# Attention and a mixing MLP in one kernel: the second batch's keys and queries turned by DMA transposes, and the order of the last product's tiles

## The chip, the cores and the metric

The kernel runs on one core of a Trainium2 chip. The metric is the device time of one launch in microseconds (us), the median of several runs. A core has TensorE (PE in the profile; its weight loads are PEld), VectorE (DVE), ScalarE (ACT), GpSimd (POOL) and SyncE (SP), and 16 DMA engines that all of its queues share. SP issues DMAs on the hardware queue that the profile calls q1, GpSimd on the software queue q0, ScalarE on q10.

## The reference

Eight batches of 384 tokens. First grouped-query attention (16 query heads on 4 key/value heads, head size 64), then a two-stage residual MLP with affine layers: a mix over tokens and an MLP over channels (1024 to 4096 to 1024).

```python
scores = (q @ k.transpose(0, 1, 3, 2)) / sqrt(64)      # k, v repeated 4 times over heads
attn   = exp(scores - max) / (sum + 1e-9)
x      = heads_to_columns(attn @ v)                    # (8, 384, 1024)
a1  = alpha1 * x + beta1
tok = einsum('ts,bsd->btd', w_tok, a1)                 # 384 x 384 over tokens
u   = x + lam * tok
a2  = alpha2 * u + beta2
ch  = maximum(a2 @ w_ch1, 0) @ w_ch2                   # 1024 x 4096, 4096 x 1024
out = u + lam * ch
```

## The kernel before

Everything is bf16 on TensorE with f32 sums. The order of instructions on each engine is the order of the program (a manual schedule); semaphores between engines come only from what reads and writes which buffer.

**Stages.** Batch 0's attention comes first, alone. Then `main(0)` and `main(1)` each do the channel MLP of one batch: a hidden product (phase 0: 32 rows of 128 hidden channels, 8 matmuls of L531 each, a relu into `hT`) and a second product (phase 1: 6 units of 32 matmuls of L569, evicted by VectorE at L576 and stored). After that come three calls of `pair`, which do two batches at once with seven half-size products for each product in place of eight, out of sums of blocks of the weights and of the operands (L722 is the hidden product, L786 the second one).

**Side work between matmuls.** `main` and `pair` are generators that yield after every four or eight matmuls. Between two yields the program puts pieces of other work from a plan: `put(stage, phase, unit, function, ...)`. So the attention of batch 1 runs inside phase 1 of `main(0)`, that of batch 2 inside phase 0 of `main(1)`, and so on. For one batch the attention is, by pairs of heads `p`: `scores` (L279 on TensorE, exp on ScalarE at L288 into `es`), `av` (L315, then four VectorE operations L320 to L330 that give `xr` and the operand `a1`), `tok` (L340, then L347 and L351 on VectorE into a buffer `a`, of which there are two), a store of `xr` into `out` (`spill`, L243 on SP) and a DMA transpose of `a` into `ops` (`a2_transpose`, L362 on SP). All scores of a batch need its keys and queries with the head dimension on the partitions: `kT` and `qT`. There is one `kT` and one `qT`, one buffer `k2` and one buffer `q_raw` that the loads fill, so the loads of batch b+1 wait until batch b's have been turned.

**Turning the heads.** There are two ways in the code. `k_transpose` and `q_transpose` (L255, L265) do it on TensorE, six 128x128 transposes into PSUM at a time, which VectorE copies out (L257, L267); batches 0 and 1 use it. `flip_k` (L172) and `flip_q` (L176) are DMA transposes on SP, from SBUF to SBUF; all later batches use them. For batch 1 the plan has the transposes at units 9, 24, 28, 32, 36 and 40 of phase 0 of `main(0)`. That phase has 60 units: the first four rows were begun in batch 0's attention and give one unit each, the other 28 rows two.

**Weights.** W1 comes in 16 chunks of two rows (256 columns, 512 KB in bf16) through a ring of six slots, by GpSimd's DMAs (`load_w1`, L185), which cast from f32: when a chunk has been used, the chunk six places on is loaded. After the last of W1 for batch 0, GpSimd issues 13 blocks of W2 (`load_w2`, L189, into `arena`), and then batch 2's k, q and v (`load_next`, L508). All of these go through q0 in that order.

**Relus.** In `main` a counter `exps` says which engine does a row's relu. An exp on ScalarE sets it to 2, each row takes one off, and while it is not below 0 the relu goes to VectorE (L542), otherwise to ScalarE (L540). The third and the sixth group of scores leave their last exp to be done later: it is put into `late`, and the next `av` issues it.

**The last product.** The last call of `pair` (`last`) ends with the product `o == 4`, in which each of three token tiles `ms` gets 16 matmuls, in two halves `h` of 8. The third token tile is held in two PSUM tiles, columns 0 to 383 and 384 to 511, and each is done by itself. When a tile has its 16th, VectorE multiplies it by lam (L794) and adds it to `ends` (L795), and SP stores it (L796).

Of the kernel before, what the change touches and what calls it, by code (L numbers as in the profile page):

```python
# [12 lines left out]
def kernel(  # L13
# [21 lines left out]
    nc = tc.nc  # L35
# [14 lines left out]
    NST = S // P  # L50
# [64 lines left out]
    def by_tok(ap):  # L115
        return ap.rearrange("(p st) d -> p st d", st=NST)
# [91 lines left out]
    late, exps = [], [0]  # L208
# [20 lines left out]
    def side(b):  # L229
# [175 lines left out]
        def av(p):  # L405
            av_piece(p, 0)
            av_piece(p, 1)
            while late:
                late.pop(0)()

        def tok_flip(p):
            tok(p)
# [18 lines left out]
        if not first:  # L431


            turns = {}
            if b == 1:
                turns = {5: [(to_all, 3, 0, 0), (load_row_set, 1, 1, 0)], 7: [(to_all, 3, 1, 1), (load_row_set, 2, 0, 1)],
                         9: [(k_transpose, 0)], 12: [(to_all, 1, 0, 2)], 14: [(to_all, 1, 1, 0), (load_row_set, 2, 1, 0)],
                         17: [(scale_beta,)], 20: [(to_all, 2, 0, 1)], 22: [(to_all, 2, 1, 0)],
                         24: [(q_transpose, 0, 2, "av")], 28: [(k_transpose, 2)]}
                for i in range(3):  # L440
                    turns[32 + 4 * i] = [(q_transpose, 2 + 2 * i, 2, "av")]
            if (b - NPL) // 2 > 0:
                at = {}

                def put(k, *m):
                    at.setdefault(k, []).append(m)

                for j in range(6):
                    put((0, 6, 12, 21, 26, 31)[j], scores3, j, j in (2, 5))
                for p in range(NP):  # L450
                    put((4, 10, 14, 18, 24, 29, 33, 35)[p], av, p)
                    put((8, 15, 17, 22, 27, 32, 36, 38 if b % 2 else 39)[p], tok_flip, p)
                    if by_pe(p):
                        put((36, 39, 41)[p - NP + 3], turn, p)
                return turns, at
            return turns, {
                0: [(scores3, 0)], 4: [(av, 0)], 6: [(scores3, 1)], 8: [(tok_flip, 0)], 11: [(av, 1)],
                13: [(scores3, 2, True)], 15: [(av, 2)], 16: [(tok_flip, 1)], 18: [(tok_flip, 2)], 19: [(av, 3)],
                21: [(scores3, 3)], 23: [(tok_flip, 3)], 25: [(av, 4)], 27: [(scores3, 4)], 29: [(tok_flip, 4)],
                31: [(av, 5)], 33: [(scores3, 5, True)], 35: [(av, 6), (tok_flip, 5)], 37: [(av, 7)],  # L460
                38: [(tok_flip, 6)], 41: [(tok_flip, 7)],
                **{39 + 4 * i - i // 2 * 2: [(turn, p)] for i, p in enumerate((5, 6, 7)) if by_pe(p)}}
# [207 lines left out]
    def pair(i):  # L670
        b0 = NPL + 2 * i
# [24 lines left out]
        last = i == NB - 1  # L696
# [12 lines left out]
        for g in range(NH // 2):  # L709
            X, Y, snap = {}, {}, {}  # L710
            for k, (o, e) in enumerate(SEQ1):
                t = 2 * g + e
# [51 lines left out]
        X = [c_banks(ms) if last else None for ms in range(NST)]  # L764
        snap = {}
        where = {2: (0, 0), 3: (0, 1), 7: (1, 1), 4: (1, 0)}
        for k, o in enumerate(PLACE2):
            whole = not last and o != 4
            for h in range(1 if whole else 2):
                for ms in range(NST):  # L770
                    if o == 4 and not last and 1 < 3 * h + ms < 5:
                        sum_w1(0, (5, 7, 6)[3 * h + ms - 2])
                    if last and (o, h) in ((6, 1), (7, 0)):
                        (lift_end if o == 7 else begin_end)(ms)
                    if last and (o, h, ms) == (7, 0, NST - 1):
                        X[ms] = [(c0, c1, pairs[sc].tile([P, 2, 512], f32, tag="sc", name="C", bufs=1)[:, 0, :c1 - c0])
                                 for sc, c0, c1 in (("sc1", 0, 384), ("sc2", 384, 512))]
                    if whole:
                        X[ms] = [(0, 512, acc.tile([P, 512], f32, tag="acc", name="C", bufs=2))]
                    elif not last and h == 0:  # L780
                        X[ms] = c_banks(ms)
                        pairs["held"] = ms == NST - 1
                    upto = NH if whole else 8 * h + 8
                    for (c0, c1, x), t in ((c, t) for c in X[ms] for t in range(8 * h, upto)):
                        slot, rhs = w2_slots[i, 4 * k + t // 4], w2_at[i, 4 * k + t // 4]
                        nc.tensor.matmul(out=x, lhsT=hid[:, t, LEFT2[o], ms * P:(ms + 1) * P],  # L786
                                         rhs=rhs[:, t % 4 * 512 + c0:t % 4 * 512 + c1],
                                         start=((not last or o in (1, 6, 7)) and t == 0), stop=(t == NH - 1),
                                         skip_group_check=True)
                        if t % 4 == 3 and ms == NST - 1 and c1 == 512 and not (o == 4 and slot >= RING):  # L790
                            free(slot)
                        if last and o == 4 and t == NH - 1:
                            e, v = ends[ms][:, c0:c1], spare(ms).bitcast(f32)[:, c0:c1]
                            tt(out=v, in0=x, in1=lam_t[:, c0:c1], op=MUL)  # L794
                            tt(out=e, in0=e, in1=v, op=ADD)  # L795
                            nc.sync.dma_start(out=by_tok(out[b0 + 1])[:, ms, c0:c1], in_=e)  # L796
                        if t % 4 == 3 and t < upto - 1 and c1 == 512:
                            q = 4 * ms + t // 4
                            if whole and o in (2, 6) and q in (2, 5, 8, 10):
                                sums_hid(o, (2, 5, 8, 10).index(q))  # L800
                            if t % 8 == 3 and later and (last or later[0][1] != 4):
                                flush(1)
                            yield 1
                    if k == ms == h == 0:
                        pad_free[:] = [RING + 1, RING + 2, RING]
                        pump()
                    if (whole or h == 1) and not (last and o == 4):
                        if o in (1, 6, 5):
                            q = ((1, 6, 5).index(o) * NST + ms) * 512
                            snap[o, ms] = snaps[:, q:q + 512]  # L810
                        else:
                            bb, dw = where[o]
                            t = snap[1, ms] if o == 7 else spare(ms).bitcast(f32)
                        for c0, c1, x in X[ms]:
                            if o == 1:
                                nc.scalar.copy(out=snap[o, ms], in_=x)
                            elif o in (6, 5):
                                tt(out=snap[o, ms], in0=x, in1=snap[1 if last or o == 6 else 6, ms], op=ADD)
                            elif o == 2 and last:
                                tt(out=t, in0=x, in1=lam_t[:, :512], op=MUL)  # L820
                            else:
                                base = {2: 1, 3: 1 if last else 5, 7: 5, 4: 6}[o]
                                tt(out=t[:, c0:c1], in0=x, in1=snap[base, ms][:, c0:c1], op=ADD)
                            if o == 7 and not last:
                                tt(out=snap[6, ms], in0=x, in1=snap[6, ms], op=ADD)
                        if o not in (1, 6, 5):
                            later.append((scaled, o, b0 + bb, ms, dw, t))
                    if last and o in (2, 6) and (h, ms) in ((0, 1), (0, 2), (1, 0), (1, 1)):
                        sums_hid(o, [(0, 1), (0, 2), (1, 0), (1, 1)].index((h, ms)))
                    yield 1  # L830
# [5 lines left out]
    with tc.manual_schedule(engines=order):  # L836
# [131 lines left out]
        def put(ps, phase, at, *m):  # L968
            plan.setdefault((ps, phase, at), []).append(m)

        def put_all(ps, phase, table, at=lambda u: u):
            for u, ms in table.items():
                for m in ms:
                    put(ps, phase, at(u), *m)

        def put_flips(ps, phase, b, places):
            for u, m in zip(places, ((flip_k, b), *((flip_q, b, i, 2) for i in range(0, NP, 2)))):
                put(ps, phase, u, *m)

        turns, at = side(1)  # L980
        put_all(0, 0, turns)
        put_all(0, 1, at)
        put_flips(0, 1, 2, (34, 36, 37, 42, 43))

        put(0, 1, 45, load_next, 3)
# [71 lines left out]
```

## Time and profile before

| | us |
|---|---|
| median of 3 runs | 740.92 (740.89 to 741.25) |
| the profiled execution, its own time | 740.56 |
| its span, first to last instruction | 738.8 |
| TensorE busy | 731.5 (99%) |
| VectorE busy | 516.9 (70%) |
| ScalarE busy | 324.1 (44%) |
| GpSimd busy | 163.5 (22%) |
| DMA moved | 151.32 MB, 205 GB/s on average |

The granted TensorE clock is 0.999 over the span. Times inside the span count from its first instruction. In the profiled execution the hidden product of batch 0 runs from about 36 to 75 us, its second product to about 130, those of batch 1 to 242, and the three pairs to the end. In a row of the timeline the columns are start, duration, engine, line, operation, out<-in, count, and in brackets the engine's idle time before it with what ended it. In a row of the DMA view's queues they are packets, MB, and the time that the packets took as a share of the 16 engines' time, which can exceed 100% because an engine has more than one packet under way.

### The profile page before, as it was taken

The numbers are of one execution on the slowest core, as the hardware profiler recorded it, in microseconds if no ns is written. First come the engines' busy times: TensorE is split into PE (matmuls) and PEld (weight loads), VectorE is DVE, ScalarE is ACT, GpSimd is POOL, SyncE is SP. The second block draws the span as 40 slices with busy tenths as digits, with TensorE's granted clock in tenths as the row PEclk, the third lists the DMA queues.
The fourth block names the chain that finished last, engine by engine and source line by source line (L and its number), as shares of the span: only waits on it lengthen the run. The fifth ranks groups of instructions, "written<-read, shape, count | busy, mean of one in ns | idle before, by whom it ended". The sixth has DMA issues, their size and how long they took to land.

```text
span 738.8 us, 14511 instructions
## 1 busy us (share of the span) xinstructions
PE 731.5 (99%) x5769; PEld 418.8 (57%) x5769; DVE 516.9 (70%) x995; ACT 324.1 (44%) x467; POOL 163.5 (22%) x211
## 2 busy tenths in 40 slices
PE   8999999999999999999999999999999999999997
PEld 5866555566555566655555566655555566654444
DVE  7763366467587889749777988847968988762354
ACT  7632431444333566653334366664343266660000
POOL 9434221420000232211013244020002222000011
PEclk9999999999999999999999999999999999999999
DMA  9999999999899999999989999998989999937965
GB/s 184 194 202 200 207 209 175 185 191 199 204 258 281 177 218 212 268 249 205 297 197 197 202 149 191 204 246 198 274 236 172 211 127 145 172 117 261 293 182 103
DMA packets 218017, 151.32 MB, mean 205 GB/s; under 512 B 88660, under 2 KB 197060, under 8 KB 217948
## 3 DMA queue, kind: packets, MB, share of 16 engines
q0 software_dynamic: 120304, 64.60, 66.6%
q1 hardware_dynamic: 97100, 85.39, 42.9%
q8 instruction: 45, 0.74, 0.4%
q10 hardware_dynamic: 544, 0.39, 0.2%
q14 instruction: 24, 0.20, 0.1%
HBM read 154.84 MB, written 38.27 MB: 261 GB/s over the span
## 4 chain that ended last, share of the span: by engine, by line
PE 95%; DVE 2%; DMA 1%; ACT 0%; issue 0%; DVEq 0%
PE C L786 30%; PE X L722 17%; PE h L531 10%; PE ch L569 10%; PE Y L722 8%; PE sc L279 5%; PE Z L722 4%; PE sc L315 4%; PE sc L340 3%; DMA ops<-a 1%; PE h L223 1%; PE tok L340 1%; PE av L315 0%; PE warm L841 0%; PE tp L265 0%; ACT hT L288 0%
## 5 line engine op out<-in xcount | busy, mean ns | idle before, releaser
L288 ACT ACTIVATE es<-sc 128x1024 bf16<-128x1024 f32 x126 | 121.4, 1023 | 155.9 <-PE sc L279 144.8
L786 PE MATMUL C<-w,arena 128*128 128x512 bf16 (+2 forms) x744 | 168.0, 372 | 0.0
L786 PEld LDWEIGHTS <-arena 128*128 128x128 bf16 x1040 | 94.8, 98 | 100.5 <-issue 5.1
L727 ACT ACTIVATE hT<-X,bias 128x384 f32<-128x384 f32 x144 | 83.7, 581 | 61.6 <-PE X L722 54.9
L722 PEld LDWEIGHTS <-w 128*128 128x128 bf16 x768 | 75.1, 98 | 50.0
L516 POOL DMA_DIRECT2D out_dram<-hT x33 | 28.7, 871 | 284.3 <-DVE hT L687 106.3
L569 PE MATMUL ch<-arena,hT 128*128 128x512 bf16 x384 | 90.8, 379 | 0.0
L185 POOL DMA_DIRECT2D w<-in_moe_w_ch_dram x68 | 62.8, 964 | 98.4 <-PE X L722 34.4
L531 PE MATMUL h<-ops,w 128*128 128x384 bf16 (+1 forms) x480 | 83.3, 327 | 0.8 <-DVE hT L542 0.7
L722 PEld LDWEIGHTS <-pad 128*128 128x128 bf16 x576 | 56.4, 98 | 37.2
L722 PE MATMUL X<-ops,w 128*128 128x384 bf16 x384 | 70.2, 326 | 0.0
L722 PE MATMUL X<-ops,pad 128*128 128x384 bf16 x384 | 70.2, 326 | 0.0
L786 PE MATMUL C<-pad,arena 128*128 128x512 bf16 (+2 forms) x296 | 69.9, 373 | 0.0
L531 PEld LDWEIGHTS <-w 128*128 128x128 bf16 x480 | 45.4, 98 | 30.4 <-issue 2.7
L569 PEld LDWEIGHTS <-hT 128*128 128x128 bf16 x384 | 34.8, 98 | 36.8 <-issue 2.5
L347 DVE TENSOR_TENSOR xr<-sc,xr 128x384 f32<-128x384 f32 x56 | 30.9, 552 | 23.4 <-PE sc L340 23.4
L315 PEld LDWEIGHTS <-es 128*128 128x128 bf16 x1008 | 38.2, 97 | 12.4
L340 PEld LDWEIGHTS <-wtokT 128*128 128x128 bf16 x576 | 37.5, 98 | 11.8 <-DVE a L330 0.8
L279 PE MATMUL sc<-qT,kT 64*128 64x384 bf16 (+2 forms) x576 | 42.0, 272 | 0.8 <-DVE xr L323 0.3
L320 DVE RECIPROCAL rinv<-sc 128x6 f32<-128x6 f32 x56 | 10.7, 192 | 44.3 <-PE sc L315 44.1
L315 PE MATMUL sc<-v,es 128*128 128x65 bf16 x1008 | 39.8, 193 | 0.0
L722 PE MATMUL Z<-ops,w 128*128 128x384 bf16 x192 | 39.0, 326 | 0.0
(138 smaller groups left out, 911.0 us busy)
## 6 DMA issues: line engine op xcount, KB each, us to landing
w<-in_moe_w_ch_dram POOLq DMA_DIRECT2D x68, 512.0 KB, 10.3
w<-w2s SPq DMA_DIRECT2D x60, 512.0 KB, 4.3
pad<-w2s SPq DMA_DIRECT2D x24, 512.0 KB, 8.1
out_dram<-xr SPq DMA_DIRECT2D x56, 192.0 KB, 6.1
out_dram<-hT POOLq DMA_DIRECT2D x33, 256.0 KB, 5.7
arena<-in_moe_w_ch_dram POOLq DMA_DIRECT2D x16, 512.0 KB, 20.0
w2s<-arena SPq DMA_DIRECT2D x28, 256.0 KB, 5.0
q_raw<-in_q_dram POOLq DMA_DIRECT2D x28, 192.0 KB, 10.4
```

The lines of the kernel that those rows point to most:

```text
L185: nc.gpsimd.dma_start(out=w1[:, w1_slots[c]], in_=w1src[:, :, c * CW * P:(c + 1) * CW * P])
L279: nc.tensor.matmul(out=sc[:, hh, k % 4:k % 4 + n], lhsT=kT[r, 2 * p // G, BLK[hh][sk], :], rhs=qT[r, p, st:st + n, :], start=True, stop=True)
L288: nc.scalar.activation(out=e, in_=sc, func=EXP, scale=scale_qk)
L315: nc.tensor.matmul(out=av[:, hh, sq, :], lhsT=ess[k // 4][:, m % 2, k % 4, :], rhs=vb[:, sk, hk, :], start=(sk == 0), stop=(sk == NST - 1))
L340: nc.tensor.matmul(out=ps[:, tt, :], lhsT=wtokT[:, st, tt * P:(tt + 1) * P], rhs=a1s[p][:, st, :], start=(st == 0), stop=(st == NST - 1 an ...
L347: nc.vector.tensor_tensor(out=u, in0=ps, in1=u, op=ADD)
L516: nc.gpsimd.dma_start(out=at, in_=o, accum_op=ADD)
L531: nc.tensor.matmul(out=ps[:, :n], lhsT=w1[:, w1_slots[c], dt, j * P:(j + 1) * P], rhs=a2T[:, dt, :n], start=(dt == 0), stop=(dt == NDT - 1))
L569: nc.tensor.matmul(out=ps, lhsT=hT[:, nt, ms * P:(ms + 1) * P], rhs=w2[:, row(nt)[0], row(nt)[1], cs], start=(i == 0), stop=(i == NNT - 1))
L722: nc.tensor.matmul(out=ps, lhsT=tb[g, o][:, dt, e * P:(e + 1) * P], rhs=opb(LEFT1[o])[:, dt], start=(o in (1, 2, 7) and dt == 0), stop=(dt ...
L727: nc.scalar.activation(out=snap[o, e], in_=ps, func=IDENT, bias=hi if o == 5 else lo)
L786: nc.tensor.matmul(out=x, lhsT=hid[:, t, LEFT2[o], ms * P:(ms + 1) * P], rhs=rhs[:, t % 4 * 512 + c0:t % 4 * 512 + c1], start=((not last o ...
```

## The change

Batch 1's `k_transpose` and `q_transpose` leave the plan, and `flip_k` and `flip_q` for batch 1 enter it: all of k at unit 50 of phase 0 of `main(0)`, the first and second quarter of q at units 54 and 58, the third and fourth at units 3 and 9 of phase 1. In `av`, a put-off exp sets the relu counter to 1 instead of the 2 that the exp itself sets. In the last product's `o == 4`, the first half is done for two token tiles only, the third tile gets all its 16 matmuls at the end, and the store of its columns 384 to 511 is issued by ScalarE.

```diff
@@ av
             while late:
                 late.pop(0)()
+                exps[0] = 1
@@ side
             if b == 1:
                 turns = {5: [(to_all, 3, 0, 0), (load_row_set, 1, 1, 0)], 7: [(to_all, 3, 1, 1), (load_row_set, 2, 0, 1)],
-                         9: [(k_transpose, 0)], 12: [(to_all, 1, 0, 2)], 14: [(to_all, 1, 1, 0), (load_row_set, 2, 1, 0)],
-                         17: [(scale_beta,)], 20: [(to_all, 2, 0, 1)], 22: [(to_all, 2, 1, 0)],
-                         24: [(q_transpose, 0, 2, "av")], 28: [(k_transpose, 2)]}
-                for i in range(3):
-                    turns[32 + 4 * i] = [(q_transpose, 2 + 2 * i, 2, "av")]
+                         12: [(to_all, 1, 0, 2)], 14: [(to_all, 1, 1, 0), (load_row_set, 2, 1, 0)],
+                         17: [(scale_beta,)], 20: [(to_all, 2, 0, 1)], 22: [(to_all, 2, 1, 0)]}
@@ pair
             whole = not last and o != 4
+            tail = last and o == 4
             for h in range(1 if whole else 2):
-                for ms in range(NST):
+                for ms in range(NST - (tail and not h)):
...
-                    for (c0, c1, x), t in ((c, t) for c in X[ms] for t in range(8 * h, upto)):
+                    for (c0, c1, x), t in ((c, t) for c in X[ms]
+                                           for t in range(0 if tail and ms == NST - 1 else 8 * h, upto)):
...
-                            nc.sync.dma_start(out=by_tok(out[b0 + 1])[:, ms, c0:c1], in_=e)
+                            (nc.scalar if c0 else nc.sync).dma_start(out=by_tok(out[b0 + 1])[:, ms, c0:c1], in_=e)
@@ the plan
         put_all(0, 1, at)
+        put_flips(0, 0, 1, (50, 54, 58))
+        put(0, 1, 3, flip_q, 1, 4, 2)
+        put(0, 1, 9, flip_q, 1, 6, 2)
         put_flips(0, 1, 2, (34, 36, 37, 42, 43))
```

`put_flips(stage, phase, b, places)` puts `flip_k(b)` at the first place and `flip_q(b, 0, 2)`, `flip_q(b, 2, 2)`, ... at the following ones, as many as there are places.

## The prediction

> **What bounds the kernel now.** I read the page's busy shares first, then the chain of waits, then the weight loads of the first batch and the DMA engines under them, and last the end of the span.
>
> ```profile
> PE 731.5 (99%) x5769; PEld 418.8 (57%) x5769; DVE 516.9 (70%) x995; ACT 324.1 (44%) x467; POOL 163.5 (22%) x211
> PE 95%; DVE 2%; DMA 1%; ACT 0%; issue 0%; DVEq 0%
> ```
>
> TensorE is the bound and hardly ever stops: between 30 us and the end only two gaps exceed 0.1 us, 0.30 at 108.70 and 0.66 at 181.32. An instruction taken from it is worth its own time, provided nothing else becomes late. The chain, in the stretch where the six groups of transposes lie, shows their price:
>
> ```profile
> 51.26 2.61 PE h L531 x16
> 54.21 2.61 PE h L531 x16
> 57.16 2.61 PE h L531 x16
> ```
>
> Sixteen matmuls (two hidden rows) take 2.61 us, but these stretches start 2.95 apart: one group of six transposes is 0.34 us. Now the DMA engines in the same stage (the queue rows of the DMA view, 46 to 66 us, then 86.5 to 90, then 93.4 to 95.8; packets, MB, sum of packet times):
>
> ```profile
> q0 software_dynamic: 7779, 3.92, 144.7%
> ...
> q0 software_dynamic: 728, 0.72, 124.3%
> ...
> q0 software_dynamic: 376, 0.37, 91.8%
> q1 hardware_dynamic: 377, 0.10, 30.0%
> ```
>
> q0 is GpSimd's queue (W1, W2, next q, k, v), q1 is SP's. In the first row W1 alone moves in 512-byte packets: 20 us x 16 engines / 7779 = 41 ns each. In the second W2's 1024-byte packets alone take 3.5 x 16 / 728 = 77 ns. In the third one transpose of an a tile (128x384 bf16, 384 packets of 256 bytes) runs beside W2: the queues take turns one for one (376 to 377), and a pair costs 2.4 x 16 / 377 = 102 ns. So a transposing packet adds 25 ns to what waits on q0. Beside the 384-byte packets of v and q, 114.2 to 114.9 us, a pair is 56 ns where such a packet alone is 33 (30 to 32 us): 23 ns added. Transposes with the engines to themselves (133.9 to 134.9) pass 1080 packets in 1 us, 15 ns each. The engines have no free time here: the page's DMA share stands at 9 tenths.
>
> How close is W1 to late? The sixteenth chunk (its issue and the matmuls in the timeline, then its landing in the DMA view):
>
> ```profile
> 59.41 0.87 POOL L185 DMA_DIRECT2D w<-in_moe_w_ch_dram  x1 [2.08 <-PE h L531]
> 62.89 12.58 PE L531 MATMUL h<-ops,w 128*128 128x385 bf16 x76
> w<-in_moe_w_ch_dram POOLq DMA_DIRECT2D x1, 512.0 KB, 11.2
> ```
>
> It is issued at 59.41 and lands 11.2 later, at 70.65. The run of 76 matmuls ends issuing at 75.30, and the chunk holds the last 16 of them: needed at 72.69. Its slack is 2.04 us. Chunks land every 2.65 us while TensorE without transposes wants one every 2.61: the transposes sit in time that the DMA engines need anyway.
>
> **The change, part by part.** *Transposes off TensorE.* Six groups x 0.34 = 2.04 us of matmul time, and six evictions of about 0.555 us (L257, L267) on VectorE, which waits there for TensorE anyway. By itself that brings the end of the hidden stage forward by 2.04, exactly to where the sixteenth chunk arrives: 70.65 + 2.61 = 73.3.
>
> *Transposes onto SP.* One of k (128x1536 bf16 = 1536 packets of 256 bytes) and four of q (128x768, 768 packets each). When do they start? The plan puts them at units 50, 54 and 58, but a place in SP's stream holds nothing back unless SP is busy:
>
> ```profile
> 41.34 4.36 SPq L924 DMA_DIRECT2D rows<-in_moe_alpha_dram  x2
> 86.64 0.65 SPq L243 DMA_DIRECT2D out_dram<-xr  x1
> ```
>
> SP has nothing from 45.7 to 86.6. k, q and v of batch 1 have landed by 36.5, and batch 0's scores read kT and qT for the last time at 24.2. So the k flip and three q flips (the one at unit 3 of the second product too, since SP waits for nothing before it) go out at about 45.7 to 53, ahead of much of W1's queue rather than behind it. Their packets start some 4 us after issue, as the store issued at 86.64 did (the first q1 packets lie at 90.7).
>
> These are 1536 + 3 x 768 = 3840 packets. At 24 ns (the rows 23 and 25; W1's 512 bytes lie between) the 16 engines lose 3840 x 24 / 16 = 5.8 us; with 65 ns a pair they pass 246 per us, so they are through at 49.7 + 15.6 = 65.3, before the sixteenth chunk lands. It lands at 76.4 instead of 70.65; the hidden stage ends at 79.0 against 75.3: **+3.7 us**, the 2.04 saved already inside. Bounds: at 15 ns +1.6, at 25 ns +4.0; if they cost nothing, -2.0. W2 stands behind W1 in q0 and moves back by 5.8 too: its (0,2,1) block lands at 78.3 + 5.8 = 84.1 and is wanted by the product's 19th matmul (the run from 77.02 on, 0.216 each: 80.0) + 3.7 = 83.7: **+0.3** (0 to 1).
>
> *The fifth flip* stands at unit 9, behind the store of the first token tile at unit 8, so SP issues it near 88.7 (times without the shift above). q1 is then a line of stores and transposes that share the engines with W2:
>
> ```profile
> 87.38 1.31 SPq L362 DMA_TRANSPOSE ops<-a  x1
> ...
> 97.30 0.60 SPq L243 DMA_DIRECT2D out_dram<-xr  x1
> 97.95 1.30 SPq L362 DMA_TRANSPOSE ops<-a  x1
> ...
> 97.95 9.35 DMA ops<-a
> ...
> 108.70 0.39 PE sc L279 x4
> ...
> DVE a L351 <- DMA ops<-a: 2.1, 1, 2.1
> ```
>
> (SP's timeline, then the chain, then the waits of 105 to 110 us.) The transpose issued at 97.95 is 9.35 us on its way, VectorE waits 2.1 for its buffer (a has two), and TensorE's 0.30 gap at 108.70 is the end of that wait. Another 768 packets at 377 per 2.4 us are 4.9 us in front of it; q1 stands idle only 1.3 us in between (100.1 to 101.4, 13 packets). So it lands 3.6 later, and as TensorE already waits at that point: **+3.6** (0 if the line has more give than I see, 4.9 with no idle time used). The flip itself is in time: about 102 for scores at 108. GpSimd's loads of batch 2's q now wait for it, until about 102 instead of 91.6, but their data stands behind W2 in q0 until 108 anyway: nothing.
>
> *Relus.* Only the hidden product of batch 1 has both relus and put-off exps: two of them, so two relus of 0.61 move to ScalarE. The gap at 181.32 is released by the relu at 180.65, the first after the exp, which stays on VectorE; the second (181.78) is the one that moves, and nobody waits for it. Nothing, bounds -0.3 and +0.1.
>
> *The tail.* The last 384-column chunk and the 128-column chunk behind it come back to back:
>
> ```profile
> 734.62 0.55 DVE L794 TENSOR_TENSOR hT<-C,vecs 128x384 f32<-128x384 f32 x1
> 735.21 0.56 DVE L795 TENSOR_TENSOR ends<-ends,hT 128x384 f32<-128x384 f32 x1
> 735.68 0.28 DVE L794 TENSOR_TENSOR hT<-C,vecs 128x128 f32<-128x128 f32 x1
> 736.00 0.29 DVE L795 TENSOR_TENSOR ends<-ends,hT 128x128 f32<-128x128 f32 x1
> ```
>
> The small matmuls issue 56 ns apart and end at 735.0, but VectorE gets to them at 735.68. Afterwards 16 of them (0.9 us) follow the wide chunk instead of 8, and VectorE's 512-column work is done 1.75 us earlier; the last eviction starts near 735.25: -0.45. The last store goes by ScalarE's queue, past the 384-column one: -0.05 more. **-0.5** (-0.7 to 0, if that queue starts slower).
>
> Sum: 3.7 + 0.3 + 3.6 + 0 - 0.5 = +7.1 us. The profiled execution took 740.56 (span 738.8 and 1.8 around it), so 747.7; the median of the runs, 740.92, is 0.36 higher: 748.0. A measurement of this kernel tells about 0.2% (1.5 us) from no change.
>
> **Rivals.** *Only W1 is hit*: the line on q1 gives way, term 3.6 becomes 0: 744.4. For: q1 has one idle stretch. Against: the chain runs through that very transfer. 0.13.
>
> *Transposes cost by bytes, not by packets.* At the rate of the lone stretch (1080 x 256 bytes in 1 us, 276 GB/s) the early 0.98 MB take 3.6 us: +1.6; the fifth flip takes 0.7, less than the idle 1.3: 0. With the tail 742.0, no change. Against it: the 102 ns pair. 0.09. The Trainium skill, Advanced Engine Details and Errata, section X-Bar Transpose (TRN2), speaks for this one: it calls transposing DMAs as fast as regular ones and expects 350 to 400 GB/s. By that an estimate of 2.5 to 2.8 us for the early flips leaves some +0.3 in all, 741.2; the trace beside W2 disagrees, with 0.10 MB of transposes in 2.4 us.
>
> *W1 has room* (faster). The packet times add up to 145% of the engines' time, so packets overlap; if the 256-byte ones slip into that overlap, W1 is not late and the 2.04 us and the tail are won: 738.4. It decides at 2.04 us of delay to the sixteenth chunk, 8.5 ns per packet. No row has transposes beside 512-byte packets; both neighbouring rows say 23 or more. 0.10.
>
> *The flips do wait for their place*, about 68 us. W1 is spared, but k's flip then needs 4 us and 1536 packets at 157 per us: landed at 82, q's first at 87, and scores are due at 74.4. Some 12.6 us of waiting less 2.0: 751 to 753. Nothing in the trace holds SP. 0.08.
>
> **How the numbers follow.** The forecast has 0.60: 748.0, its own range 742 to 751. To hold 8 in 10 I start at 741.5, which takes in the rival by bytes, and end at 751; the faster case and the latest flips stay out. Faster 0.11, same 0.08, slower 0.81.
>
> **What would show it.** DMA transposes on SP at 46 to 53 us; the sixteenth W1 chunk landing near 76; matmuls of L531 waiting for w in the chunks after the eighth; the first product starting near 79; VectorE waiting 5 us for ops<-a around 111 to 115; last DVE eviction without a queue ahead of it. I am wrong if L531 never waits for DMA, or if the flips first appear after 65 us.

## The result and the profile after

| | before | changed |
|---|---|---|
| median of 5 runs each, us | 740.89 (740.31 to 741.25) | 750.49 (748.80 to 752.07) |
| ratio, 95% interval | | 1.0127 (1.0110 to 1.0145) |
| profiled execution, its own time | 740.56 | 752.07 |
| its span | 738.8 | 750.3 |

The change makes the kernel 9.6 us slower by the medians. The profiled execution happened to be the slowest of the five, 11.5 above the one of before, so the traces have 1.9 us more to explain than the medians.

The page of the changed kernel, busy shares and chain of waits:

```profile
PE 728.6 (97%) x5674; PEld 416.4 (56%) x5733; DVE 511.4 (68%) x987; ACT 325.4 (43%) x469; POOL 163.6 (22%) x211
...
PE 77%; DMA 9%; DVE 5%; issue 5%; POOL 3%; ACT 0%; POOLq 0%; DVEq 0%
```

TensorE's recorded work is 2.9 us less (36 transposes are gone, and 59 of its 5733 matmuls have no record in this trace), and yet the span grew: where transfers were 1% of the chain they are 9%. VectorE has 8 instructions fewer (six evictions, two relus), ScalarE two more.

Where the time went, by stages of the traces (each stage from its first matmul to that of the next; us):

| | before | changed | difference |
|---|---|---|---|
| hidden product of batch 0 | 38.60 | 42.78 | +4.2 |
| second product of batch 0 | 55.69 | 62.37 | +6.7 |
| hidden product of batch 1 | 56.52 | 55.78 | -0.7 |
| second product of batch 1 | 55.55 | 55.73 | +0.2 |
| hidden product of the second pair | 72.80 | 74.1 | +1.3 |
| from the last product's first matmul to the end | 76.55 | 76.30 | -0.3 |

**First stage.** SP's timeline of the changed kernel:

```profile
45.69 3.44 SPq L172 DMA_TRANSPOSE kT<-k  x1
49.23 9.69 SPq L176 DMA_TRANSPOSE qT<-q_raw  x3
...
93.26 2.29 SPq L176 DMA_TRANSPOSE qT<-q_raw  x1
...
102.51 1.29 SPq L362 DMA_TRANSPOSE ops<-a  x1
```

Four flips go out the moment SP is free, at 45.7, not at the 68 us of the units that they were put behind. The DMA view under them, 53 to 65 us (packets, MB, sum of packet times), and the sixteenth chunk, issued at 60.83 (the DMA view of 60.8 to 60.9, with the time to landing at the end):

```profile
q0 software_dynamic: 2923, 1.47, 88.6%
q1 hardware_dynamic: 2928, 0.73, 46.5%
```

```profile
w<-in_moe_w_ch_dram POOLq DMA_DIRECT2D x1, 512.0 KB, 16.1
```

One packet of W1, one of the flips: 12 us x 16 / 2925 = 65.6 ns a pair, where a W1 packet alone took 41. The chunk lands at 76.97 instead of 70.65. The chain and TensorE's waits (36 to 80 us) show what that does:

```profile
47.77 18.46 DMA w<-in_moe_w_ch_dram
...
66.27 13.53 PE h L529 x80
```

```profile
PEld L529 <- DMA w<-in_moe_w_ch_dram: 7.9, 8, 2.0
...
PE h L529 <- DMA w<-in_moe_w_ch_dram: 5.2, 4, 1.6
```

TensorE stops four times, 5.2 us in all, before the ninth to the twelfth chunk. The last stop is for the *twelfth* (issued 47.77, landed 66.23): behind it 80 matmuls, five chunks, run to 79.80 without a further one on this list. They are not ahead of the loads, though: the weight loads (PEld) wait eight times, once for each chunk from the ninth to the sixteenth, and in the single records the first matmul of each of these starts 0.05 us after its landing, that of the sixteenth at 77.01. So the loads set the pace to the end of the stage.

**Second stage.** The chain, then rows of the timeline, 107 to 150 us:

```profile
102.51 12.82 DMA ops<-a
...
117.34 3.25 PE ch L567 x8
```

```profile
115.42 0.56 DVE L351 TENSOR_TENSOR a<-xr,vecs 128x384 bf16<-128x384 f32 x1 [4.97 <-DMA ops<-a]
...
116.74 0.61 PE L279 MATMUL sc<-qT,kT 64*128 64x128 bf16 x4 [3.81 <-DVE xr L323]
...
140.10 0.34 PE L428 MATMUL sc<-ident,a 128*128 128x128 bf16 x3 [1.18 <-DVE a L351]
```

The transpose of an a tile issued behind the fifth flip needs 12.82 us. VectorE waits 4.97 for its buffer, TensorE stands 3.81, and a second time, at 140, VectorE waits 3.42 and TensorE 1.18. One line of the chain is in no term of the forecast: eight matmuls in 3.25 us, where the same eight take 1.83 elsewhere in this chain. The stretches before and in it (us, busy of PE, PEld, DVE, ACT, POOL, then the granted clock, DMA share, GB/s):

```profile
112.90:116.70 3.80, 0.03 (x2) 0.00 (x0) 1.22 (x3) 1.85 (x2) 0.74 (x1) 1.00 1.40 190
116.80:120.40 3.60, 3.60 (x12) 1.20 (x13) 1.03 (x2) 1.02 (x1) 1.48 (x2) 0.53 1.30 221
```

After 3.8 us without work the granted clock is 0.53 over 3.6 us; in narrower stretches it is 0.50 from about 116.75 to 120.16, 3.41 us, and 1.00 again behind that. Matmuls follow each other at 427 ns instead of 216, about seven times: 1.5 us more.

**The tail.** VectorE's timeline at the end:

```profile
745.90 0.56 DVE L794 TENSOR_TENSOR hT<-C,vecs 128x384 f32<-128x384 f32 x1 [1.19 <-PE C L786]
...
747.28 0.29 DVE L795 TENSOR_TENSOR ends<-ends,hT 128x128 f32<-128x128 f32 x1
```

VectorE is now idle when the third token tile arrives (1.19 us). Counted from the last product's start, its last instruction ends 0.47 earlier; but the store that ScalarE issues at 747.60 takes 2.7 us to the end of the span where SP's took 2.5, so a quarter of a us is left.

### The profile page after: what moved, and what is told of

Read it like the earlier page. It is cut to its first block, busy times and chain, and to the rows that moved or that the text cites. A ratio compares the mean times of both kernels' runs of the same rounds, so it can differ in the third digit from the quotient of the medians.

```text
span 750.3 us, 14388 instructions
## 1 busy us (share of the span) xinstructions
PE 728.6 (97%) x5674; PEld 416.4 (56%) x5733; DVE 511.4 (68%) x987; ACT 325.4 (43%) x469; POOL 163.6 (22%) x211
## 4 chain that ended last, share of the span: by engine, by line
PE 77%; DMA 9%; DVE 5%; issue 5%; POOL 3%; ACT 0%; POOLq 0%; DVEq 0%
PE C L786 26%; PE X L720 14%; PE ch L567 9%; PE h L529 7%; PE Y L720 7%; DMA w<-in_moe_w_ch_dram 4%; PE sc L279 4%; PE sc L315 4%; PE Z L720 3%; PE sc L340 3%; DMA ops<-a 3%; DMA q_raw<-in_q_dram 2%; POOL w L185 1%; DVE xr L323 1%; DVE a1f L328 1%
## 5 line engine op out<-in xcount | busy, mean ns | idle before, releaser
L786 PE MATMUL C<-w,arena 128*128 128x512 bf16 (+2 forms) x711 | 163.7, 372 | 1.6 <-issue 0.3
L786 PEld LDWEIGHTS <-arena 128*128 128x128 bf16 x1040 | 94.7, 98 | 100.6 <-issue 5.1
L786 PE MATMUL C<-pad,arena 128*128 128x512 bf16 (+2 forms) x288 | 69.5, 373 | 0.4
L720 PE MATMUL Y<-ops,w 128*128 128x384 bf16 x192 | 39.0, 326 | 0.9 <-DVE arena L733 0.9
```

Source lines behind the costliest of these rows:

```text
L720: nc.tensor.matmul(out=ps, lhsT=tb[g, o][:, dt, e * P:(e + 1) * P], rhs=opb(LEFT1[o])[:, dt], start=(o in (1, 2, 7) and dt == 0), stop=(dt ...
```

## The experiments

### Which part costs: the flips, the relus, the tail

*tail_relu* is the changed kernel with the TensorE transposes of before in place of the flips; *relu_only* is the kernel before with one line.

```diff
# tail_relu, against the changed kernel
+                         9: [(k_transpose, 0)], ...
+                         24: [(q_transpose, 0, 2, "av")], 28: [(k_transpose, 2)]}
+                for i in range(3):
+                    turns[32 + 4 * i] = [(q_transpose, 2 + 2 * i, 2, "av")]
-        put_flips(0, 0, 1, (50, 54, 58))
-        put(0, 1, 3, flip_q, 1, 4, 2)
-        put(0, 1, 9, flip_q, 1, 6, 2)
# relu_only, against the kernel before
+                exps[0] = 1
# flips_only, against the changed kernel: av and pair as before
-                exps[0] = 1
-            tail = last and o == 4
...
```

> Only the tail and the relu counter are changed; batch 1's heads are turned on TensorE as before. Theory (all of the loss comes from the transposes on SP): the tail gives -0.3 as in the changed kernel's trace, and the relus give -0.5 to -0.7, because there the gap of 0.66 before the hidden row at 181 us nearly went; about 740.0, -0.1%. Rival (the tail's new order or the store on ScalarE's queue costs): 741.2 or more.

Measured: 739.96 against 740.54, ratio 0.9990 (0.9981 to 0.9998). The two small parts together are a gain of 0.6 us.

> Only the relu counter after a put-off exp is set to 1. Prediction's step: nothing (740.9, the relu that moves is not the one that TensorE waits for). Rival from the changed trace: the relu on ScalarE frees a PSUM bank sooner and the next row takes that bank, so the 0.66 gap at 181 us shrinks to about 0.1: 740.3.

Measured: 740.44 against 740.54, ratio 0.9996 (0.9986 to 1.0006): not to be told from no change in the total. In the stage it shows. The timeline of relu_only where before had a gap of 0.66:

```profile
180.10 0.58 ACT L541 ACTIVATE hT<-h,bias 128x384 bf16<-128x384 f32 x1 [1.61 <-PE h L532]
...
180.60 0.61 DVE L543 TENSOR_SCALAR hT<-h,bias 128x384 bf16<-128x384 f32 x1
...
180.73 1.46 PE L532 MATMUL h<-ops,w 128*128 128x384 bf16 x8
```

TensorE's next row starts 0.05 after *ScalarE's* relu ends (180.10 + 0.58), while VectorE's relu is still running: by these times the row takes the PSUM bank that ScalarE frees, and the 0.66 is about 0.1. That it is this line's doing shows in all traces: a gap of 0.65 or 0.66 behind a VectorE relu stands in each of the six kernels without the line (before, none, k_by_dma, flips_only, fifth_added_again, half_added) and in none of the seven with it. The stage as a whole tells less, because other waits fall into it: it takes 55.78 to 56.36 in five kernels with the line and 56.74 and 57.33 in the two with a third buffer (below), 56.31 to 57.29 in the six without.

> Only the move of batch 1's heads to SP; tail and relus as before. Theory: the whole loss and a little more, since the small gains of tail and relus are missing: about 751.3. Rival (part of the loss comes from tail or relus): below 749.5.

Measured: 752.02 against 740.39, ratio 1.0156 (1.0141 to 1.0171). The flips are the whole loss, +11.6. The change lost 9.6, and the small parts by themselves win 0.6; the 1.4 left over are not explained (the changed kernel's five runs lie 3.3 us apart).

### Is the fifth flip's place what costs in the second product?

*fifth_early* issues the fifth flip behind the fourth, while SP has nothing else. *fifth_added* does the opposite: nothing of the change but one q flip at unit 9, in addition to TensorE's transposes (it writes the same values again). *half_added* adds half of that flip, 384 packets.

```diff
# fifth_early, against the changed kernel
-        put(0, 1, 9, flip_q, 1, 6, 2)
+        put(0, 1, 3, flip_q, 1, 6, 2)
# fifth_added, against the kernel before
+        put(0, 1, 9, flip_q, 1, 6, 2)
# half_added, against the kernel before
+        put(0, 1, 9, flip_q, 1, 6, 1)
```

> The changed kernel with the fifth flip at unit 3 of the second product, ahead of the first store, so that all five go out early. Theory (two separate places): W1 is delayed by 4608 packets at 26 ns, 7.5 us, hidden stage +5.4; the line on SP's queue at 95 to 112 us is as it was before, so no gap of 3.8 us at the fourth pair's scores and no slow clock after it: about 746.5. Rival (what counts is how many packets go by DMA before 125 us, wherever they stand): 750.5 as the changed kernel. Rival (the gap comes from W2 and the stores running late, not from the fifth flip): 751.5 or more.

Measured: 746.61 against 740.39, ratio 1.0084 (1.0069 to 1.0099). TensorE's gap is back at 0.40 (0.30 before), the second product takes 55.93 (before 55.69), and what stays is mainly the first stage, 43.67. VectorE's longest wait for ops<-a is 2.2 us.

> The kernel before with the fifth flip added at its place, beside TensorE's own transposes (it writes once more what stands in qT). W1 is not touched. Theory: the transposes of a behind it land 3.6 later, VectorE waits, TensorE stops for 3.9 us, and its clock is granted at about half for the next 3.4 us (+1.5): 746 to 747. Rival (the line has give, or transposes cost by bytes): 740.9 to 741.5.

Measured: 745.80 against 740.39, ratio 1.0071 (1.0055 to 1.0088). Its profiled execution took 1962 us, with matmuls more than twice as long as elsewhere (those of L786 811 ns on average, 372 before) at a recorded clock of 1.00. Nothing here explains it; it is left out, and *fifth_added_again* is the same kernel once more.

> The same kernel as fifth_added, for a trace: VectorE waits some 4 to 5 us for ops<-a near 111, TensorE stands for 3.5 to 4 us before the fourth group of scores, and the granted clock is about 0.5 for the 3.4 us behind it. Rival: a gap without a slower clock, and a second gap later.

Measured: 745.08, one run. The second product takes 60.28, +4.6, with W1 untouched (first stage 38.60, exactly as before). VectorE waits 4.57 for ops<-a until 109.98. The timeline row of the gap, and the stretch behind it:

```profile
111.29 0.61 PE L279 MATMUL sc<-qT,kT 64*128 64x128 bf16 x4 [3.52 <-DVE xr L323]
```

```profile
111.30:114.70 3.40, 3.40 (x13) 1.22 (x14) 1.08 (x2) 1.02 (x1) 0.74 (x1) 0.58 1.29 208
```

> The kernel before with half of the fifth flip added at the same place (one pair of heads, 384 packets). Theory: 2.4 us of queue less 1.3 of idle time, a gap of 1.1 to 1.5 us, too short for the clock to drop: 742.0 to 742.4. Rival (in proportion, with no idle time to absorb and no threshold): half of what the whole flip costs, 743.6.

Measured: 742.22 against 740.39, ratio 1.0025 (1.0015 to 1.0034). VectorE's wait is 2.9 and TensorE's gap 1.11; the second product is 0.8 longer, and the last store adds another 0.8 in this trace, so that the median falls into the forecast's 742.0 to 742.4 is in part luck. The stretch after the gap keeps the full clock:

```profile
109.16 0.39 PE L279 MATMUL sc<-qT,kT 64*128 64x128 bf16 x4 [1.11 <-DVE xr L323]
```

```profile
110.00:113.40 3.40, 3.40 (x24) 1.79 (x23) 1.40 (x3) 0.79 (x1) 1.03 (x2) 1.00 1.43 211
```

Half a flip makes the gap 0.8 longer, a whole one 3.2, and only the long gap brings the slow clock. How long the clock stays low is not the same each time. In flips_only the gap is 3.89, hardly longer than the changed kernel's 3.81, but the clock is at half from 115.43 to 122.26:

```profile
116.30:122.20 5.90, 5.90 (x24) 2.66 (x25) 1.83 (x4) 1.02 (x1) 1.48 (x2) 0.50 1.37 209
```

It was at half for 3.41 us in the changed kernel and in fifth_added_again, 6.83 in flips_only and 13.65 in held (below), once, twice and four times 3.41, and it fell 2.9 to 5.4 us after the last matmul. The Trainium skill, TensorE: Matmul & The Clock Gate, Part 1 (the HAM clock gate), says that an idle window of about 3.4 us halves TensorE's clock, that a busy one restores it, and that the windows run freely. The traces agree, the multiples of 3.41 above all; a gap of 1.11 is followed by 1.00. So the price of a gap depends on where it falls: of the half-clock time 3.4 and 2.8 us fell on work in the changed kernel and in fifth_added_again, 6.0 in flips_only and in held; half of that, an estimate, is 1.4 to 1.7 us against 3.0. In flips_only the second gap of the changed kernel, at 140, is missing in return, and its second product is as long (62.36).

### Is a packet the price, and what is the slack of W1?

*k_by_dma* flips k only (1536 packets) and leaves q to TensorE. *none* turns nothing: batch 1's scores read batch 0's turned heads, so the computation of batch 1 is not done as the reference asks; only its time is of interest.

```diff
# k_by_dma, against the kernel before
-                         9: [(k_transpose, 0)], 12: ...
-                         24: [(q_transpose, 0, 2, "av")], 28: [(k_transpose, 2)]}
+                         12: ...
+                         24: [(q_transpose, 0, 2, "av")]}
+        put(0, 0, 50, flip_k, 1)
# none, against the kernel before: 9, 24, 28 and the loop over i leave the plan
```

> Only the keys go by SP (one flip of 1536 packets, free to start at about 45.7 us); the queries stay on TensorE. Theory by packets (26 ns each, the rate of the changed kernel): W1 is delayed by 2.5 us against 2.04 of slack, the hidden stage ends 0.5 later: 741.4. Rival by bytes (0.39 MB at 276 GB/s, 1.4 us, inside the slack): the two groups of transposes are won, -0.7: 740.2.

Measured: 743.93 against 740.54, ratio 1.0046 (1.0030 to 1.0062): slower than either theory. The chain, 36 to 80 us:

```profile
42.42 15.46 DMA w<-in_moe_w_ch_dram
...
58.76 0.33 PE tp L265 x6
...
64.99 12.41 PE h L531 x76
```

TensorE waits for the *tenth* chunk, issued at 42.42 before the flip and landed at 57.89 instead of 54.79. In the kernel before, the tenth chunk's first matmul starts 1.2 us after the landing (56.01), the sixteenth's 2.04: the slack grows with the transposes in between, and a chunk that is late here has not yet got that of the sixteenth. Three groups of transposes, 1.0 us, still come behind it. The stage is 40.51, +1.9. The sixteenth chunk is 3.2 us later: 3.2 x 16 / 1536 = 33 ns for each packet of the first flip, against 26 over all four (6.3 x 16 / 3840). The rest of this trace's loss lies in two places, 0.8 in the hidden product of batch 1 (a wait of 0.81 for a transposed tile) and 0.8 at the last store, which took 3.3 instead of 2.5 us although nothing there differs; fifth_added_again and half_added have the same 0.8 at the end.

> Batch 1's keys and queries are not turned at all: neither on TensorE nor by SP, so its scores use batch 0's turned heads; this leaves out work. Theory (the sixteenth W1 chunk has 2.04 us of slack and TensorE cannot run ahead of it): -2.0, 738.9, with L531 rows waiting for w near the end of the hidden stage by no more than 0.1 to 0.2 us each. Rival (W1 binds already with the transposes in): no gain, 740.9. Rival (the transposes also held something else): below 738.3.

Measured: 740.78 against 740.54, ratio 0.9999 (0.9990 to 1.0007). The chain of its first stage:

```profile
36.69 36.59 PE h L528 x224
```

224 matmuls without one stop, 36.59 us, 2.0 less than before: the saving is real in its stage. In the median it doesn't appear. In the traced execution (739.47, the second fastest of twelve) the span is 1.2 shorter, and some is given back: 0.2 in the next product, 0.4 in the hidden product of batch 1, 0.3 in that of the second pair. Where the rest goes in the median run was not settled (see the end).

### What if the flips did keep their place?

*held* moves four pieces of VectorE's and SP's set-up work to unit 48 and behind it, so that SP is kept busy until 67.9 and the flips go out behind W1's loads.

```diff
-                         12: [(to_all, 1, 0, 2)], 14: [(to_all, 1, 1, 0), (load_row_set, 2, 1, 0)],
-                         17: [(scale_beta,)], 20: [(to_all, 2, 0, 1)], 22: [(to_all, 2, 1, 0)]}
+                         12: [(to_all, 1, 0, 2)], 20: [(to_all, 2, 0, 1)],
+                         48: [(to_all, 1, 1, 0), (load_row_set, 2, 1, 0)], 49: [(scale_beta,)], 58: [(to_all, 2, 1, 0)]}
```

> The changed kernel with a row load on SP put at unit 48 (behind a copy on VectorE at that unit), so that SP cannot issue the flips before about 66 us: they really stand behind W1's loads. Theory (no place is free, the engines are full until 125 us): W1 is spared, the hidden stage ends near 73.5, but the first scores wait for the second flip until about 85, TensorE's clock drops once more, and the line on SP is as late: 753 to 757. Rival (behind W1 they cost less than ahead of it): below 750.

Measured: 753.32 against 740.22, ratio 1.0171 (1.0153 to 1.0190). The chain of 66 to 100 us, and the stretches behind the wait:

```profile
72.11 15.53 DMA qT<-q_raw
...
87.69 1.46 PE sc L279 x12
```

```profile
87.70:91.10 3.40, 3.40 (x17) 1.48 (x17) 0.00 (x0) 2.77 (x3) 0.74 (x1) 0.50 1.22 196
91.20:95.00 3.80, 3.80 (x19) 1.58 (x18) 0.00 (x0) 0.00 (x0) 1.43 (x2) 0.67 1.21 194
```

W1 is spared (first stage 37.35, less than before), and the first scores wait for q until 87.69; the clock, at half since 80.04, stays there until 93.70. Behind the loads the flips come too late, ahead of them they make the loads late.

### Does one more buffer for a take the second stall away?

*after_a3* gives batch 1 three `a` buffers in place of two, in a part of `ops` that is free then; *tail_relu_a3* is tail_relu with the same.

```diff
+    def a2_third(p):
+        at = 3456 + p % 3 * S
+        return ops[:, at:at + S].rearrange("p (a d) -> p a d", a=NST)
-            a2s[p] = next_a2() if b > NPL + 1 else sb.tile([P, NST, P], bf, tag="a2", name="a2", bufs=2)
+            a2s[p] = next_a2() if b > NPL + 1 else a2_third(p) if b == 1 else sb.tile([P, NST, P], bf, tag="a2", name="a2", bufs=2)
```

> The changed kernel with three buffers in place of two for a, the operand that waits for its DMA transpose (batch 1 only; they lie in a free part of ops). The transposes on SP are as late as in the changed kernel, but VectorE need not wait for the one issued at 102. Theory (the buffer's wait is what stops TensorE at 116.7): the 3.8 us gap and the slow clock behind it go, the hidden stage's 4.3 stays: 744.5 to 745.5. Rival (the wait for the product's store at 108.6, 3.0 us, or another one on the same late queue takes its place): 748 or more.

Measured: 747.09 against 740.22, ratio 1.0082 (1.0067 to 1.0097). The gap and the slow clock are gone (second product 56.49), so the wait for the buffer, not for the flipped q, was what stopped TensorE. The stretch in which the changed kernel had the half clock:

```profile
115.00:120.00 5.00, 4.09 (x40) 2.19 (x38) 2.92 (x6) 0.53 (x1) 1.48 (x2) 1.00 1.34 213
```

But of 5.9 us won in that stage the median shows 3.4. Against the changed kernel its trace gives back 1.6 in the hidden product of batch 1 (57.33), 0.6 in the first stage (43.41) and 0.3 in the hidden product of the second pair. In the first of these TensorE waits 0.97 at 138.9 for a transpose into `ops`; this may be the changed kernel's second stall, 1.18 at 140.1, in another form and behind the border of the stage, which no run separates.

> Tail and relu counter as in the changed kernel, heads turned on TensorE, and three buffers for a. Theory: the 0.30 gap at 108.7 us of the kernel before goes as well: 739.7, faster than the kernel before by 0.1%. Rival: no difference to tail and relu alone, 740.0.

Measured: 739.63 against 740.22, ratio 0.9988 (0.9979 to 0.9998). It has the lowest median of all and beats both kernels, before by 0.1%; from tail_relu (0.9990) it can't be told. The 0.30 gap is gone, as expected (second product 55.21, in tail_relu 55.85), but the hidden product of batch 1 takes 0.95 more, with a new wait of 0.80 for a transpose at 132.6.

## Why the prediction was right

The forecast was 748.0 with a range to 751, the measured median 750.49. Direction, both places and both mechanisms are as foretold; the size was 2.5 us short. That the median still lies inside the range is partly luck: the losses with a dash in the table, which the forecast did not have, come to 4.7 us, and the traced execution, 752.07, lies outside. Term by term, against the trace of the changed kernel:

| term | forecast | trace |
|---|---|---|
| flips ahead of W1, transposes saved | +3.7 | +4.2 |
| W2 block late | +0.3 | no wait for it |
| fifth flip: TensorE's gap | +3.6 | +3.5 (3.81 - 0.30) |
| slow clock behind the gap | - | +1.5 |
| second gap, 140 us | - | +1.2 |
| rest of the second product | - | +0.5 |
| relus | 0 | -0.7 |
| second product of batch 1 | - | +0.2 |
| hidden product of the second pair | - | +1.3 |
| tail | -0.5 | -0.3 |
| sum | +7.1 | +11.4 |

**Right: the early flips.** Issue at 45.7, first packets 4 us later, one-for-one turns at 65.6 ns a pair (65 forecast), 26 ns a packet (24), the sixteenth chunk at 76.97 (76.4), the stage's end at 79.6 (79.0), though SP is busy issuing until 58.9, not 53. The step "needed at 72.69, slack 2.04" holds for the whole change: the sixteenth chunk is waited for, and its 16 matmuls end the stage. But it looked at one chunk alone. A slack of 2.0 to 2.2 us is true only of the thirteenth to the sixteenth; by the first matmul behind each landing in the kernel before, the seventh to the twelfth have 0.8, 0.8, 1.0, 1.2, 1.6 and 1.9. In the changed kernel the twelfth to the sixteenth are all 6.2 to 6.3 us late, more than any slack, so the choice did no harm. In k_by_dma the chunks are some 3 us late and the tenth decides: the same reasoning, applied to that kernel, missed by 2.5 us.

**Right: the fifth flip's gap; mis-sized: what a gap costs.** 12.8 us under way, 4.97 of waiting, 3.81 of gap against 3.9 forecast. The sum priced a gap at its own length. In this one the clock fell to half, and that is 1.5 us more; it fell in all four kernels with a gap of 3.5 us or more, for 1.4 to 3.0 us of loss, and in none behind the gaps of up to 1.6. The second wait for the same buffers, 1.2 us, was overlooked: the forecast followed the line on q1 only to the first stop.

**Wrong: that nobody waits for the relu; mis-sized: the tail.** Two relus moved, as said, and the one at 180.6 stayed on VectorE, as said. "Nobody waits for it" was wrong: which of two banks is free first changed, and the next row took the earlier one; -0.7 lies outside the bounds of -0.3 and +0.1. (The prediction's "only two gaps exceed 0.1 us" passes over one of 0.14 at 153.65; nothing hangs on it.) In the tail VectorE is done 0.47 earlier (0.45 forecast), but the store on ScalarE's queue is 0.2 slower, not 0.05 faster.

**Not borne out in the total: the saved 2.04 us.** The sum counts them as won wherever nothing else costs ("if they cost nothing, -2.0"). In none the stage is indeed 2.0 shorter, but the median of the runs is not lower than before.

**The rivals.** By bytes falls on q1: half a flip made TensorE's gap 0.8 us longer and a whole one 3.2, so the second 384 packets cost 2.4, as they would at one turn each (2.4 us for 377), where their 0.1 MB takes 0.4 at 276 GB/s and would have fitted into the idle time. For what the flips take from W1 the two counts are not so far apart: at W1's own rate here, 3.92 MB in 20 us or 196 GB/s, the 0.98 MB would take 5.0 us and k's 0.39 MB 2.0, against 6.3 and 3.2 measured; only the rate of 276 GB/s that the rival assumed is clearly too fast. The sentence of the Trainium skill (Advanced Engine Details and Errata, X-Bar Transpose (TRN2)) that stood beside it does not hold for transposes beside a full queue either: next to W1 the flips moved 0.73 MB in 12 us, 61 GB/s, and what they took from the queue beside them, 25 ns for 256 bytes on each of 16 engines, is 164 GB/s, not 350. "W1 has room" falls with the four stops. Flips that wait for their place cost 753.3 in held (751 to 753 forecast), but here they didn't wait (issued at 45.7). "Only W1 is hit" is what fifth_early became: 746.6, with 768 more packets ahead of W1 than the 744.4 assumed.

**Open.** The +1.3 in the second pair. The chain of the changed kernel (450 to 470 us) leads to a W1 chunk that is 15.06 us on its way, through VectorE's sums of its blocks to TensorE's gap of 0.90 at 465.71:

```profile
444.96 15.06 DMA w<-in_moe_w_ch_dram
...
465.71 0.81 PE Y L720 x4
```

The same gap is 0.90 in after_a3 (and one of 0.36 ahead of it), 0.48 in flips_only, 0.17 in none, and absent before and in fifth_early. So it isn't bound to the flips (none has no flips at all). A load that lands with no room to spare would explain that 2 us won or lost early do not arrive whole at the end, and the scatter of the runs (738.80 to 741.88 in none); no run varied it, so that stays an argument. With it stays open what becomes of none's 2 us in the median run.

## What to carry to other kernels

A place in the program holds a DMA back only if its queue has something to wait for before it (45.7 us here, 67.9 where SP was kept busy): look at when the issuing engine is idle, and expect the transfer there. Where two queues share full DMA engines, count their packets: here they took turns one for one. Take the slack of every chunk and not only of the last one. In these traces a gap on TensorE cost its length up to 1.6 us, and 1.4 to 3.0 us more from 3.5 us on, so a stall that can't be removed is better split in two, an inference from the gaps here that no run tried by itself.

## What the runs showed that was not expected

- Behind gaps of 3.81 and 3.89 us the half clock lasted 3.41 us in one kernel and 6.83 in another, so nearly the same stall has two prices.
- The first flip's packets cost W1 33 ns each, the following ones 3.1 us for 2304, 22 ns: soon after the start of the first flip both queues run slow for about 0.5 us, near 51.5 us, which explains only a part of it.
- From issue to the end of the span SP's last store took 2.5 to 3.3 us in the seven kernels with the old tail, which are alike there: 0.8 us, more than the tail's whole gain. ScalarE's took 2.7 in all six with the new one.
